# One weight fetch moved to the head of its period, and the GpSimd weight sums begun one period later

## The chip, the cores and the metric

The kernel runs on one core of a Trainium2 chip. The metric is the device time of the whole program in microseconds (us). Before the change it is 1308.43 us, the median of three runs (1307.17 to 1308.57).

## What is computed

The reference has two parts. The first is attention with a threshold over 8 batches of 8 heads, with 576 queries and keys of 64 elements each:

```
scores = q @ k.T / 8
scores = where(scores >= max(scores) - tau, scores, -1e9)
attn   = exp(scores - max) / (sum + 1e-9)
x      = attn @ v            # then (B,H,S,D) -> (4608, 512)
```

The second is a feed-forward layer on the 4608 rows of x: `h = max(x @ w_in, 0)`, then `out = (h * h) @ w_out`, with w_in 512 x 2048 and w_out 2048 x 512. The weights arrive with 64 bits per element, all else with 32.

## The kernel before, in words

**Two stages.** The attention stage runs to about 512 us of the span, and the feed-forward stage fills the rest. The feed-forward stage multiplies with a two-level scheme of seven products in place of eight (49 products of sums of blocks for each layer), so it needs sums of weight blocks and sums of x beside the blocks themselves. The weights must be turned into 32-bit floats first. Both of these are done in the shadow of attention.

**Periods.** Two heads of one batch make a pair (32 pairs). A unit is up to 128 query rows of a pair, and a period `p` of the function `period` handles two units, A and B (the lists stand from L592 on, `period` itself at L619). There are 72 periods with scores, from 0 to 71, and a few before and after that fill and drain the pipeline. A period issues its work in the order of a list of step names, and each engine executes its instructions in exactly that order. `BEGIN_WITH` has lists for periods 0 and 1, `CONVERTING` is the list while weights are converted (periods 2 to 34), and `PLAIN` is the list after that. The steps that matter here are:

- `SA`, `SB`: scores of unit A and B on TensorE (L434). `topA0` to `topB1`: the maximum over keys on VectorE (L452). `powA0` and so on: the exponential on ScalarE (L462). `maskA0` and so on: the threshold, product and row sum on VectorE (L467). `leastA`, `leastB` (L459) and `over` (L474): tiny GpSimd operations that make the threshold and the sum's denominator. `inv`: the reciprocal on VectorE (L477).
- `U`, `V`, `W`: transposes of the weights of attention on TensorE (L380, and L515 for the reciprocal). `eU`, `eV`, `eW`: their copies out of PSUM on ScalarE (L523). `PV`: the product with v on TensorE (L532). `x`: the result out of PSUM, on ScalarE (L657) in converting periods and on VectorE (L659) in plain ones. `xm`: the scaling on GpSimd (L669, converting periods alone).
- `T`, `eT`: the turn (transposes, L398) of a q or a k block of a later pair, and its copies (L403, L411). Behind `eT` the loads of q (L294) or of k and the rests of q (L308, L315, L316) for the pair two ahead are issued. Seven DMAs make one pair's k. The k of pair 2 is turned in period 3, the q of pair 2 in period 2.
- `fetch`: the load of weight chunk `p` in period `p` (L191), 128 x 512 elements of 64 bits, 512 KB. Four places hold raw chunks.
- `c1` to `c6`: the conversion of a chunk. Chunk m has `c1` (ScalarE, L205), `c3` (GpSimd, L219) and `c2` (GpSimd, L212) in period m + 2, and `c4`, `c5` (VectorE, L227 and L235) and `c6` (GpSimd, L245) in period m + 3. The 32 chunks start in periods 2 to 33, so the last one ends in period 34.
- `s1`, `s2`: one sum of weights each on GpSimd (L122 or L125, 128 x 512), in periods for which `sums_due` says yes. From period 60 on only `s1` makes one. The queue of sums holds 44 for w_in and, appended in period 44, 12 for the first block of x.

All loads and stores but the first few are issued by one engine, SyncE (SP), in the order of the text. Each DMA takes one of eight semaphores in turn, so a DMA waits until the one eight places ahead of it has landed.

In the list of period 1 the fetch of chunk 1 stands behind `eT`, and so behind the loads of k for pairs 2 and 3 that `eT` issues. `sums_due` holds from period 35 on, since `max(starts)` is 33 and period 34 still converts.

Of the kernel before, what the change touches and what calls it, by code (L numbers as in the profile page):

```python
# [48 lines left out]
def kernel(  # L49
# [512 lines left out]
    starts = {m + 2: m for m in range(16 + EARLY)}  # L562
# [2 lines left out]

    def sums_due(p):

        return p > max(starts) and not converts(p)

    def sums_step():  # L570
        while summing and next(summing[0], 0) == 0:
# [11 lines left out]
    def converts(p):  # L583
        return is_wide and (has_chunk(p) or has_chunk(p - 1))

    def has_chunk(p):
        return p in starts

    def begun(n):
# [15 lines left out]
            maskA0 maskA1 maskB0 maskB1  # L605
        """.split(),
        1: """
            SA SB T eT fetch over topA0 topA1 leastA inv V topB0 topB1 leastB powA0 powA1 eV W
            powB0 eW maskA0 maskA1 powB1 maskB0 maskB1
        """.split(),  # L610
    }
# [7 lines left out]
    def period(p):  # L619
# [67 lines left out]
        def every(key):  # L687
# [10 lines left out]
            "c3": lambda: convert3(begun(p)), "c4": lambda: convert4(begun(p - 1)),  # L698
            "c5": lambda: convert5(begun(p - 1)), "c6": lambda: convert6(begun(p - 1)),
            "s1": lambda: sums_due(p) and sums_step(), "s2": lambda: sums_due(p) and p < 60 and sums_step(), "fetch": lambda: fetch(begun(p + 2)),  # L700
        }
        steps["over"] = lambda: do(a, "over")
# [536 lines left out]
```

## Time and profile before

| what | us |
|---|---|
| median of three runs | 1308.43 |
| profiled execution, its own time | 1308.95 |
| its span (first to last instruction) | 1307.2 |
| attention stage, up to the first product of the feed-forward stage | 512.5 |
| TensorE busy | 1283.6 (98% of the span) |
| VectorE, ScalarE, GpSimd busy | 1010.1, 846.1, 915.6 |
| granted TensorE clock, mean | 0.995 |

All times of rows are counted from the start of the span. In a timeline a row gives its start, its duration, the engine and line, the operation, out<-in with shapes and a count where several were merged; brackets tell how long the engine was idle before the row and what ended the wait. SPq is SyncE's queue, whose rows are issues of DMAs. A window row gives the busy time of each engine in a stretch (instructions in brackets), then the granted TensorE clock (1.00 is full speed), the share of the DMA engines and their GB/s. A time to landing runs from the start of a DMA's issue to the arrival of its data.

Where the start of a period is spoken of below, it is the start of the first of its four maximum rows (L452) on VectorE. By these rows converting periods last 7.05 to 7.09 us from period 5 to 33 (one of 7.17 apart), and plain ones 6.34 to 7.15 us from period 36 on, in a pattern that returns every nine periods.

### The profile page before, as it was taken

Reading aid. Unit: us, or ns where it says so; the run is one execution under the profiler, and the core shown is the slowest. Engines: PE = TensorE matmul, PEld = TensorE weight load, DVE = VectorE, ACT = ScalarE, POOL = GpSimd, SP = SyncE. Lnnn points to the kernel's source line nnn. Section 1 sums busy time; section 2 is a strip of 40 time slices with the busy share of each in tenths; the row PEclk is TensorE's granted clock in tenths of the full one; section 3 lists DMA queues with packets and bytes.
Section 4 is the critical chain, followed back from the end, with each engine's and each line's share of the span. In section 5 each row is a group of like instructions: output and inputs, shape, how many; then the busy total and the mean of one; then the engine's idle time right before and its main releaser. Section 6 shows DMA issues by size and latency. Waiting matters only on the chain.

```text
span 1307.2 us, 47836 instructions
## 1 busy us (share of the span) xinstructions
PE 1283.6 (98%) x19463; PEld 1158.4 (89%) x19463; DVE 1010.1 (77%) x2431; ACT 846.1 (65%) x1498; POOL 915.6 (70%) x1023
## 2 busy tenths in 40 slices
PE   8899999999999999999999999999999999999998
PEld 5677777777777778999999999999999999999998
DVE  6899999999999996877787778777646654665463
ACT  5999999988999985657665766675523432433240
POOL 2778788765555320978897889768777777777775
PEclk8999999999999999999999999999999999999999
DMA  5665666544433313466656665579645224522511
GB/s 126 165 158 144 169 180 191 147 103 101 94 78 79 81 39 80 140 192 218 195 169 194 215 196 166 176 262 396 226 157 162 72 95 159 161 65 99 161 33 33
DMA packets 247035, 192.12 MB, mean 147 GB/s; under 512 B 97184, under 2 KB 195488, under 8 KB 246816
## 3 DMA queue, kind: packets, MB, share of 16 engines
q1 hardware_dynamic: 245504, 188.66, 48.0%
q8 instruction: 153, 2.51, 0.8%
q14 instruction: 66, 0.54, 0.1%
q10 hardware_dynamic: 1312, 0.41, 0.1%
HBM read 116.65 MB, written 72.35 MB: 145 GB/s over the span
## 4 chain that ended last, share of the span: by engine, by line
PE 88%; ACT 4%; DVE 3%; DMA 2%; issue 1%; SPq 1%; POOL 0%; ACTq 0%; POOLq 0%; DVEq 0%
PE ph L840 29%; PE po L975 29%; PE sc L532 10%; PE sc L434 10%; PE pt L380 5%; DVE arena L452 2%; PE sc L515 2%; PE sc L398 2%; ACT arena L462 2%; ACT arena L523 1%; PE sc L380 1%; DMA wall<-w 1%; DMA arena<-in_q_dram 1%; DMA g<-arena 0%; DMA arena<-in_moe_w_in_dram 0%
## 5 line engine op out<-in xcount | busy, mean ns | idle before, releaser
L125 POOL TENSOR_TENSOR arena<-arena 128x512 f32<-128x512 f32 (+1 forms) x314 | 377.8, 1222 | 134.9 <-DVE arena L125 116.6
L975 PE MATMUL po<-wall,arena 128*128 128x128 f32 x3528 | 395.0, 276 | 1.8 <-ACT arena L752 1.4
L975 PEld LDWEIGHTS po<-wall,arena 128*128 128x128 f32 x3528 | 394.3, 192 | 2.4 <-ACT arena L752 1.8
L840 PE MATMUL ph<-arena,wall 128*128 128x128 f32 x3528 | 394.2, 275 | 0.7 <-DVE arena L659 0.7
L840 PEld LDWEIGHTS ph<-arena,wall 128*128 128x128 f32 x3528 | 394.0, 192 | 0.8 <-issue 0.8
L125 DVE TENSOR_TENSOR arena<-ph,arena 128x512 f32<-128x512 f32 x378 | 256.4, 689 | 86.2 <-PE ph L840 66.3
L122 POOL TENSOR_TENSOR arena<-arena 128x128 f32<-128x128 f32 (+2 forms) x314 | 254.8, 812 | 48.8 <-DMA arena<-w 32.6
L467 DVE SCALAR_TENSOR_TENSOR arena<-arena 128x576 f32<-128x576 f32 x288 | 236.5, 857 | 2.2 <-ACT arena L462 1.3
L125 DVE TENSOR_TENSOR arena<-po,arena 128x128 f32<-128x128 f32 x378 | 108.3, 290 | 167.9 <-PE po L975 163.7
L452 DVE TENSOR_SCALAR_CACHE_REDUCE arena<-sc 128x576 f32<-128x576 f32 x288 | 205.2, 748 | 12.3 <-ACT arena L523 4.1
L462 ACT ACTIVATE arena<-arena 128x576 f32<-128x576 f32 x288 | 208.8, 774 | 8.1 <-DVE arena L452 5.1
L786 ACT COPY c<-arena 128x512 f32<-128x512 f32 (+1 forms) x303 | 173.5, 580 | 50.5 <-DVE arena L122 41.3
L532 PEld LDWEIGHTS sc<-arena 64*64 64x64 f32 x5760 | 159.2, 133 | 36.3 <-DVE arena L452 20.3
L532 PE MATMUL sc<-arena 64*64 64x128 f32 (+1 forms) x5760 | 180.4, 263 | 2.7 <-DVE arena L452 1.1
L434 PE MATMUL sc<-arena 64*64 64x64 f32 (+1 forms) x2304 | 177.5, 417 | 4.8 <-ACT arena L403 2.3
L122 DVE TENSOR_TENSOR arena<-arena,c 128x512 f32<-128x512 f32 (+1 forms) x267 | 174.9, 663 | 6.0 <-ACT c L786 4.0
L523 ACT COPY arena<-pt 128x1024 f32<-128x1024 f32 x144 | 146.2, 1016 | 29.7 <-PE pt L380 28.4
L752 ACT COPY arena<-po 128x128 f32<-128x128 f32 x63 | 16.6, 263 | 186.5 <-PE po L975 183.7
L380 PEld LDWEIGHTS pt<-ident,arena 64*128 64x128 f32 x2304 | 84.0, 140 | 40.9 <-ACT arena L523 28.3
L752 ACT COPY arena<-ph 128x512 f32<-128x512 f32 x63 | 36.6, 581 | 124.2 <-PE ph L840 123.7
L434 PEld LDWEIGHTS sc<-arena 64*64 64x64 f32 x2304 | 74.4, 134 | 42.7 <-issue 15.5
L380 PE MATMUL pt<-ident,arena 64*128 64x64 f32 x2304 | 102.8, 230 | 3.2 <-ACT arena L523 2.2
(51 smaller groups left out, 917.6 us busy)
## 6 DMA issues: line engine op xcount, KB each, us to landing
g<-arena SPq DMA_DIRECT2D x144, 256.0 KB, 2.5
arena<-g SPq DMA_DIRECT2D x144, 256.0 KB, 4.5
w<-arena SPq DMA_DIRECT2D x60, 256.0 KB, 2.4
wall<-w SPq DMA_DIRECT2D x49, 256.0 KB, 5.2
arena<-w SPq DMA_DIRECT2D x44, 256.0 KB, 3.0
arena<-in_v_dram SPq DMA_DIRECT2D x32, 288.0 KB, 3.9
out_dram<-arena SPq DMA_DIRECT2D x70, 128.0 KB, 2.2
arena<-in_q_dram SPq DMA_DIRECT2D x64, 128.0 KB, 3.8
```

Of the source, the lines that this page charges most:

```text
L122: e.tensor_tensor(out=out, in0=x, in1=y, op=ALU.subtract)
L125: e.tensor_tensor(out=out, in0=x, in1=y, op=ALU.add)
L380: made = nc.tensor.transpose(pt[:, r, ts(slot, HALF)], of[rows, :], ident[rows, rows])
L434: made = nc.tensor.matmul(sc[at, ds(to, count)], lhs, kT[rows, ds(at_k, count)], start=True, stop=True)
L452: made = nc.vector.tensor_scalar(out=s[:, j, :], in0=sc[:, ds(at, S)], scalar1=1.0, scalar2=None, op0=ALU.mult, op1=ALU.min, accum_out=nmx ...
L462: nc.scalar.activation(out=w[:, :, j, :], in_=of(j), func=AF.Exp, bias=nmx[:, j : j + 1], scale=-1.0)
L467: nc.vector.scalar_tensor_tensor(out=w[:, :, j, :], in0=of(j), scalar=thr[:, j : j + 1], in1=w[:, :, j, :], op0=ALU.is_le, op1=ALU.mult, a ...
L523: touch("weights", nc.scalar.copy(joined(to), whole(pt, 0, count)), at, 2 * BANK, m)
L532: made = nc.tensor.matmul(sc[ds(u * D, D), ds(5 * j * BANK + row, count)], loaded_v[i][rows, (c - (u != j)) % CH, :], wT[m][rows, ds(weigh ...
L786: nc.scalar.copy(c, y)
L840: nc.tensor.matmul(to[:, j, :], W_IN[m, k][:, ts(j, P)], of[k][:, m - 1, :], start=(not more and j == 0), stop=True, skip_group_check=True,)
L975: nc.tensor.matmul(to, g[:, j, :], w[:, j, :], start=(not more and j == 0), stop=(j == 3), skip_group_check=True)
```

## The change

Two lines change. In the list of period 1, `fetch` moves from the fifth place to the first. In `sums_due`, the bound rises by two, so that the first sums are made in period 36 in place of 35 (period 34 was excluded anyway).

```diff
     def sums_due(p):
-        return p > max(starts) and not converts(p)
+        return p > max(starts) + 2 and not converts(p)
...
         1: """
-            SA SB T eT fetch over topA0 topA1 leastA inv V topB0 topB1 leastB powA0 powA1 eV W
+            fetch SA SB T eT over topA0 topA1 leastA inv V topB0 topB1 leastB powA0 powA1 eV W
             powB0 eW maskA0 maskA1 powB1 maskB0 maskB1
         """.split(),
```

The instructions of TensorE, VectorE and ScalarE keep their order. On SP the issue of chunk 1 moves ahead of fourteen issues, the k loads of pairs 2 and 3, and stands right behind the four q loads of these pairs. On GpSimd the 56 sums stay in their order, and the first of them stands one period later among the tiny operations of attention. The last stands two periods later, since the final sums come one to a period.

## Prediction, made before the changed kernel was run

> **What bounds the kernel now.** First the chain that ended last, by engine:
>
> ```profile
> PE 88%; ACT 4%; DVE 3%; DMA 2%; issue 1%; SPq 1%; POOL 0%; ACTq 0%; POOLq 0%; DVEq 0%
> ```
>
> TensorE carries the end. Work on other engines counts only where TensorE or the chain of attention waits for it, and time saved before 512 us reaches the end, because from there on TensorE is busy throughout (its waits behind 495 us add up to 3.8 us). So I looked for the two places the diff touches in the list of waits. Chunk 1 has one wait to its name, in ScalarE's timeline of period 3:
>
> ```profile
> 30.01 1.01 ACT L523 COPY arena<-pt 128x1024 f32<-128x1024 f32 x1
> 34.35 0.66 ACT L205 ACTIVATE arena<-arena 128x512 f32<-128x512 f32 x1 [3.33 <-DMA arena<-in_moe_w_in_dram]
> 34.91 2.09 ACT L462 ACTIVATE arena<-arena 128x576 f32<-128x576 f32 x3
> ```
>
> ScalarE is free at 31.02 and holds all its later work behind `c1` of chunk 1 (L205) until the chunk lands. TensorE's timeline shows that this is passed on, once through the reciprocal (POOL's `over` stands behind `c3`, which needs `c1`) and once through the copies of `x`:
>
> ```profile
> 33.99 0.34 PE L380 MATMUL sc<-ident,arena 64*128 64x64 f32 x4
> 36.55 0.46 PE L515 MATMUL sc<-ident,arena 64*64 64x64 f32 x16 [2.22 <-DVE arena L477]
> 38.01 1.24 PE L434 MATMUL sc<-arena 64*64 64x512 f32 x12 [1.00 <-ACT arena L657]
> ```
>
> The same hole costs once more. The granted clock (the 1.00 or 0.50 in the windows) falls right after it:
>
> ```profile
> 34.00:38.00 4.00, 0.79 (x24) 0.52 (x20) 1.68 (x6) 3.65 (x10) 2.66 (x5) 1.00 1.05 307
> 39.20:42.60 3.40, 3.40 (x46) 1.90 (x38) 2.75 (x7) 2.81 (x5) 2.66 (x4) 0.50 0.18 39
> 42.60:46.00 3.40, 3.40 (x104) 2.89 (x104) 3.01 (x9) 2.85 (x7) 2.36 (x5) 1.00 0.58 137
> ```
>
> 46 matmuls in 3.4 us at half clock, 104 in the next 3.4. The only other fall inside the kernel (18.7 to 25.5) also follows a stretch with little TensorE work (1.36 us busy of 14 to 18).
>
> The second place is period 35. Its maxima start at 260.50, those of period 36 at 268.51: 8.01 us, where the same place of the nine-period pattern takes 6.52 (period 44) and 6.51 (period 53). GpSimd, VectorE, TensorE there:
>
> ```profile
> 262.24 0.23 POOL L474 TENSOR_SCALAR arena<-arena 128x4 f32<-128x4 f32 x1
> 262.55 1.28 POOL L125 TENSOR_TENSOR wall<-wall 128x512 f32<-128x512 f32 x1
> 263.81 0.29 POOL L459 TENSOR_SCALAR arena<-arena,tau_p 128x2 f32<-128x2 f32 x1
> 264.07 1.29 POOL L122 TENSOR_TENSOR wall<-wall 128x512 f32<-128x512 f32 x1
> ```
>
> ```profile
> 264.14 1.83 DVE L467 SCALAR_TENSOR_TENSOR arena<-arena 128x576 f32<-128x576 f32 x1 [0.78 <-POOL arena L459]
> ```
>
> ```profile
> 266.23 1.51 PE L434 MATMUL sc<-arena 64*64 64x512 f32 x24 [0.90 <-DVE arena L659]
> ```
>
> GpSimd enters the first plain period late, with chunk 31's `c6` and `xm` (260.00 to 262.16). The first sum then stands ahead of `leastA`, the mask waits 0.78 for that, then meets the second sum and takes 1.83 in place of the usual 0.81, and `x` behind it (L659) makes TensorE wait 0.90.
>
> **The fetch, step by step.** SP now:
>
> ```profile
> 16.34 4.42 SPq L308 DMA_DIRECT2D arena<-in_k_dram  x2
> ...
> 24.30 0.60 SPq L316 DMA_DIRECT2D arena<-in_q_dram  x1
> 25.00 1.29 SPq L308 DMA_DIRECT2D arena<-in_k_dram  x2
> ...
> 29.60 1.68 SPq L191 DMA_DIRECT2D arena<-in_moe_w_in_dram  x2
> ```
>
> After the change the chunk takes the place of 16.34. The issue there was held 3.76 (the longest L308); a fetch's own issue takes 0.43 to 1.20, so it ends between 16.8 and 20.1. Fetches land 3.9 to 6.6 after their start (median 4.8), a start at the end of the hold included: 20.2 to 26.7. It is wanted at 31.02, so the wait goes with 4.3 us or more to spare.
>
> What is late next in period 3? ScalarE starts `c1` 3.33 earlier, so `x`'s copies let TensorE begin period 4's scores at 38.01 - 3.33 = 34.68. VectorE's last conversion row ends at 33.45, and its run of rows without idle time, 36.32 to 40.57, then begins at 33.45 and ends at 37.70. TensorE needs 2.36 from the scores through the turn (46.12 to 48.48 in period 5, at full clock): 37.04. So VectorE is later, and period 4's maxima start at 37.70 in place of 41.14: **3.44**. Period 4 lasted 7.56; without half clock I give it the 7.06 of its successors: **0.50**. Together **3.94**. Bounds: at most (10.82 - 7.06) + 0.50 = 4.26, and 3.44 if the clock falls anyway.
>
> What the moved issue pushes back: the seven k DMAs of pair 2, whose last lands at 27.1 now (24.30 + 2.8), wanted by TensorE's turn at 29.80:
>
> ```profile
> 29.80 0.47 PE L398 MATMUL sc<-ident,arena 64*128 64x64 f32 x10
> ```
>
> They slip by one issue (0.43 to 1.20) and by the chunk's 512 KB, an estimated 1.7 us at the 269 to 331 GB/s of 17 to 20 us: 27.5 to 30.0. The slack is 2.7, so I take nothing, and keep 0.2 of loss as the near bound. The q of pair 2 (issued 14.69, lands 6.75 later, TensorE waits 0.44 for it) is ahead of the chunk; shared bandwidth could cost 0 to 1.7, and I take 0, since its row now has a k load in the same place behind it. Pair 3's k (wanted in period 5) and chunk 2 have room: chunk 2 now starts at 30.85, lands 5.0 later and has one fetch less ahead of it, and is wanted at 41.68 - 3.44 = 38.2. The raw chunks have four places, so none is short. SP's eight semaphores come round as before once chunk 1 is passed.
>
> **The sums, step by step.** In period 35 GpSimd goes from `over` (262.47) straight to `leastA` (0.29), done near 262.85. The mask starts when VectorE's fourth maximum ends, 263.36, and takes 0.74, the spacing of masks in an undisturbed run: 264.10. `x` then waits for `PV`, which ends at 264.18, and ends near 264.65, before TensorE comes to need it: the scores follow L515 (264.88) at its spacing of 0.28, at 265.2 in place of 266.23. That is 1.0. Period 36 in turn took 6.94 from scores to scores (266.23 to 273.17) where its successors take 6.58 and 6.51, as it began with VectorE late: 0.4 more, less what the first sums cost there. Taken: **1.3**, between 0.9 (the wait alone) and 1.49 (8.01 - 6.52).
>
> At the other end, 44 + 12 = 56 sums were made as 25 x 2 + 6 and end in period 65; now 24 x 2 + 8, ending in period 67, near 479 us. Their user begins at 512, so 33 us cover them; otherwise the cost would be one sum, 1.3, for each that is left. Periods 66 and 67 gain a sum each: 7.13 and 6.35 without, 7.14 and 6.35 at the same places (57, 58) with three and one. Cost 0, bound 0.2 each (6.50 against 6.68 in periods 69 and 60). GpSimd's tiny operations behind the sums are the same there as in every plain period.
>
> The mask of 1.83 bears on a rule of the Trainium skill (page "SBUF — State Buffer", section "SBUF: two separate sides"): GpSimd and a VectorE operation with two SBUF inputs take a shared port pair as an exclusive lock, and the loser waits for the whole instruction. The trace agrees: 264.14 to 265.36 is the rest of the second sum, and 0.61 is left for the mask. By that rule alone the change only moves collisions.
>
> **Sum.** 3.94 + 1.3 = 5.2 us. The profiled execution: 1308.95 - 5.2 = 1303.7 (span 1302.0, with 1.75 around it). It lies 0.52 above the median of the runs shown, so the predicted median is 1308.43 - 5.2 = **1303.2**.
>
> **Rivals.**
> 1. *The collision moves along* (10%). Period 36 takes over the loss of period 35, as it also holds two sums ahead of its masks. For: a mask beside a sum took 1.83. Against: period 36 with two sums lasted 6.44 and its mask took 1.10, since GpSimd was in time. Gain 3.94 alone: 1304.5.
> 2. *k comes late* (8%). Chunk 1 delays pair 2's k beyond 29.80. For: seven issues behind, one queue of DMAs. If the chunk's issue is held to 20.10 and the first k issue ends only when the chunk has landed, 4.8 to 6.6 later (24.9 to 26.7), k's last lands 7.0 after that, as it does now (20.10 to 27.1): 31.9 to 33.7. TensorE needs it at 30.2 (the last two of the ten transposes): a stall of 1.7 to 3.5, 2.6 in the middle: 1305.8. Against: the first k issue now ends at 20.10, while the first chunk and all four q loads are still under way, so it need not wait for a landing. The Trainium skill ("DMA: Bandwidth & Descriptors", section "Queues, rings and completion order") has descriptors on one engine consumed in ring order, which speaks against this change: by it k comes later by the chunk's transfer, the 1.7 above, and still in time.
> 3. *The wait does not go* (4%), as ScalarE is held by something hidden under it (period 3's maxima, all done at 33.1). Then only the sums count: 1307.1.
> 4. *Slower* (3%). SP is held a second time: the chunk lands at 26.7, the next k issue is held 3.76 more, and k's last lands 7.0 later, at 37.5. TensorE stalls 7.3 from 30.2 on, and the half clock stays (0.50): 7.8 lost in place of 3.94, with 1.3 from the sums: +2.6, 1311.0. It turns slower once k lands behind 34.9 (30.2 + 3.94 + 1.3 - 0.5). Against: of the six k issues behind the first, the longest took 1.49.
>
> **Numbers.** Forecast 75%. This kernel's measurement can tell about 0.2% (2.6 us) from no change. Faster by more than that (below 1305.8): the forecast, rival 1 and over half of rival 2, 0.90. Within: rival 3, the rest of rival 2, 0.07. Slower 0.03. Range: the best case, 4.26 + 1.49, gives 1302.7; the lowest of the runs shown lies 1.26 under their median, so 1301.4. Above, the middle of rival 2, 1305.8.
>
> **What would show it.** Right: no wait at L205 in period 3, maxima of period 4 near 37.7, full clock from 25.5 on, period 35 near 6.6 with a mask of 0.8 and TensorE's 0.90 gone, then the same rows up to 5.2 us earlier. Wrong: a wait of L398 for k near 30, a half-clock window near 39, period 36 near 8.

## The result, and the profile after

The changed kernel takes 1303.86 us (median of five runs, 1302.09 to 1304.45), the kernel before 1308.57 beside it (1307.17 to 1309.65). The ratio is 0.9959, with a 95% interval of 0.9947 to 0.9972: a gain of 4.7 us, between 3.7 and 6.9. The forecast was 1303.2 and a gain of 5.2. The profiled execution took 1302.09 (span 1300.3), the fastest of its five, so it flatters the change, and the account below doesn't rest on it alone. One execution of the kernel before, among the comparisons below, took 2088.8 at a granted clock of 0.556 and is left out of every ratio.

The first product of the feed-forward stage starts at 506.01 in place of 512.47. From there to the first product of the second layer both kernels take 394.03 us. So 6.5 of the 6.9 by which the two profiled spans differ are gained in the attention stage, as the prediction had it.

The chain that ended last, by engine, on the page of the changed kernel:

```profile
PE 91%; ACT 4%; DVE 3%; DMA 2%; issue 1%; POOL 0%; ACTq 0%; POOLq 0%; SPq 0%; DVEq 0%
```

SyncE's queue has gone from 1% to 0%. ScalarE's timeline of period 3 in the changed kernel shows why:

```profile
28.35 1.01 ACT L523 COPY arena<-pt 128x1024 f32<-128x1024 f32 x1
29.26 0.69 ACT L205 ACTIVATE arena<-arena 128x512 f32<-128x512 f32 x1
29.84 2.10 ACT L462 ACTIVATE arena<-arena 128x576 f32<-128x576 f32 x3
```

`c1` (L205) follows the copy at once, with no bracket behind it. TensorE's timeline, same stretch:

```profile
28.14 0.47 PE L398 MATMUL sc<-ident,arena 64*128 64x64 f32 x10
...
32.50 0.34 PE L380 MATMUL sc<-ident,arena 64*128 64x64 f32 x4
32.77 0.46 PE L515 MATMUL sc<-ident,arena 64*64 64x64 f32 x16
33.05 1.36 PE L434 MATMUL sc<-arena 64*64 64x512 f32 x24
```

Both waits that `c1` had caused (2.22 at L515, 1.00 at L434) are gone, and the turn of k (L398) doesn't wait for its data, though the chunk now stands ahead of it on SyncE:

```profile
16.45 1.83 SPq L191 DMA_DIRECT2D arena<-in_moe_w_in_dram  x1
18.32 1.26 SPq L308 DMA_DIRECT2D arena<-in_k_dram  x2
...
22.24 1.44 SPq L316 DMA_DIRECT2D arena<-in_q_dram  x1
...
28.38 0.97 SPq L191 DMA_DIRECT2D arena<-in_moe_w_in_dram  x1
```

The long hold fell on the chunk's issue and was 1.83 in all. The fetches up to 39.2 land 4.6 to 5.9 after their start, where the landing is recorded, and chunk 1 is there at 22.40, 6.9 ahead of `c1`. The windows of the changed kernel (TensorE is the first pair of numbers, the granted clock the third from the end):

```profile
30.00:33.40 3.40, 3.40 (x106) 3.00 (x106) 3.40 (x11) 3.40 (x9) 2.66 (x5) 1.00 1.09 267
36.30:39.70 3.40, 3.28 (x96) 2.80 (x92) 3.40 (x11) 3.31 (x6) 3.16 (x7) 1.00 0.38 82
```

TensorE has no hole, and no half clock follows. Now periods 35 and 36, GpSimd first, then VectorE and TensorE:

```profile
257.19 0.23 POOL L474 TENSOR_SCALAR arena<-arena 128x4 f32<-128x4 f32 x1
257.52 0.29 POOL L459 TENSOR_SCALAR arena<-arena,tau_p 128x2 f32<-128x2 f32 x1
...
261.97 0.23 POOL L474 TENSOR_SCALAR arena<-arena 128x4 f32<-128x4 f32 x1 [2.77 <-DVE arena L467]
262.28 1.28 POOL L125 TENSOR_TENSOR wall<-wall 128x512 f32<-128x512 f32 x1
```

```profile
258.24 0.81 DVE L467 SCALAR_TENSOR_TENSOR arena<-arena 128x576 f32<-128x576 f32 x1
...
264.90 0.81 DVE L467 SCALAR_TENSOR_TENSOR arena<-arena 128x576 f32<-128x576 f32 x1
```

```profile
260.12 1.27 PE L434 MATMUL sc<-arena 64*64 64x512 f32 x24
```

In period 35 `leastA` (257.52) stands right behind `over`; the mask starts at 258.24 without a wait and takes 0.81, and TensorE goes into the scores without its 0.90. The first sum is at 262.28, in period 36, where GpSimd is in time; the mask there (264.90) takes 0.81 as well. Period 35 lasts 6.50 (8.01 before), period 36 lasts 6.44 (6.44 before).

### The profile page after: what moved, and what is told of

It is laid out like the page before. It is cut to its first block, busy times and chain, and to the rows that moved or that the text cites. A ratio compares the mean times of both kernels' runs of the same rounds, so it can differ in the third digit from the quotient of the medians.

```text
span 1300.3 us, 47830 instructions
## 1 busy us (share of the span) xinstructions
PE 1280.6 (98%) x19463; PEld 1157.1 (89%) x19463; DVE 1009.3 (78%) x2431; ACT 846.5 (65%) x1498; POOL 916.7 (71%) x1023
## 4 chain that ended last, share of the span: by engine, by line
PE 91%; ACT 4%; DVE 3%; DMA 2%; issue 1%; POOL 0%; ACTq 0%; POOLq 0%; SPq 0%; DVEq 0%
PE ph L840 30%; PE po L975 29%; PE sc L532 11%; PE sc L434 10%; PE pt L380 6%; DVE arena L452 2%; PE sc L515 2%; PE sc L398 2%; ACT arena L523 1%; ACT arena L462 1%; DMA wall<-w 1%; PE sc L380 1%; DMA g<-arena 0%; ACT arena L403 0%; PE idle L1027 0%
## 5 line engine op out<-in xcount | busy, mean ns | idle before, releaser
L434 PE MATMUL sc<-arena 64*64 64x64 f32 (+1 forms) x2304 | 176.5, 414 | 3.4 <-ACT arena L403 2.3
L434 PEld LDWEIGHTS sc<-arena 64*64 64x64 f32 x2304 | 74.2, 134 | 41.4 <-issue 14.4
```

Of the source, the lines that this page charges most:

```text
L434: made = nc.tensor.matmul(sc[at, ds(to, count)], lhs, kT[rows, ds(at_k, count)], start=True, stop=True)
```

## Experiments

The theory on trial: ScalarE holds all its later work behind `c1` until chunk 1 is there, and that hold, the half clock that follows it and the loss in period 35 are the whole gain. The rivals: it is the order of the DMAs that counts, not the hold; the half clock comes anyway; period 35 loses by the place of the sum in GpSimd's queue alone, or by the ports alone; and k is close to being late. Twelve runs were made, in three groups of four; each is compared with runs of the kernel before on the same chip (medians 1308.19, 1307.51 and 1307.69).

| run | time, median | ratio, 95% interval | `c1` of chunk 1 starts [wait] | from there to period 5 | half clock after 30 us | period 31 | period 35 |
|---|---|---|---|---|---|---|---|
| before (profile) | 1308.57 | 1 | 34.35 [3.33] | 14.35 | yes | 7.09 | 8.01 |
| changed (profile) | 1303.86 | 0.9959 (0.9947–0.9972) | 29.26 | 13.79 | no | 7.36 | 6.50 |
| fetch_alone | 1304.54 | 0.9969 (0.9957–0.9981) | 29.49 | 13.92 | no | 7.39 | 7.99 |
| sums_alone | 1307.58 | 0.9994 (0.9982–1.0005) | 33.87 [4.72] | 14.82 | yes | 7.07 | 6.50 |
| c1_late | 1305.73 | 0.9977 (0.9966–0.9987) | 33.16 | 11.09 | no | 7.34 | 8.00 |
| least_first | 1308.59 | 0.9998 (0.9988–1.0007) | 34.75 [5.61] | 14.67 | yes | 7.05 | 7.63 |
| hot_hole | 1313.75 | 1.0044 (1.0028–1.0059) | 31.86 [0.91] | 16.43 | no | 7.08 | 8.01 |
| three_ahead | 1302.23 | 0.9959 (0.9945–0.9974) | 29.45 | 13.66 | no | 7.08 | 6.50 |
| two_ahead | 1303.12 | 0.9965 (0.9953–0.9978) | 30.15 | 13.99 | no | 7.09 | 6.50 |
| after_again | 1302.77 | 0.9965 (0.9952–0.9978) | 29.14 | 13.98 | no | 8.79 | 6.50 |
| hot_hole2 | 1308.04 | 0.9999 (0.9990–1.0009) | 32.56 [1.80] | 13.93 | no | 7.08 | 8.00 |
| first_only | 1307.32 | 0.9996 (0.9985–1.0007) | 32.56 [3.17] | 14.68 | yes | 7.08 | 7.00 |
| three_again | 1303.24 | 0.9963 (0.9949–0.9976) | 30.17 | 13.94 | no | 7.06 | 6.50 |
| after_third | 1302.59 | 0.9965 (0.9953–0.9978) | 30.28 | 13.88 | no | 7.70 | 6.51 |

All columns from the fourth on are read from one profiled execution each, the lengths from the starts of the maxima as before. Between 10 and 30 us every one of the fourteen profiles has one stretch of half clock, which begins between 16 and 20 us. It lasts 3.4 us in eight of them and 6.8 in six (the profile before, hot_hole, hot_hole2, two_ahead, three_again, after_third). Period 3 starts at 28.46 to 29.27 in the eight and at 29.96 to 30.49 in the six. Both lengths occur with the old and with the new place of the fetch: the three profiles of the changed kernel have 3.4, 3.4 and 6.8. So the shorter periods 1 and 2 of its first profile go with the shorter half clock and not with the change.

**fetch_alone**: the list of period 1 alone.

```diff
-            SA SB T eT fetch over topA0 topA1 leastA inv V topB0 topB1 leastB powA0 powA1 eV W
+            fetch SA SB T eT over topA0 topA1 leastA inv V topB0 topB1 leastB powA0 powA1 eV W
```

> Only the fetch of chunk 1 moves to the head of period 1; the sums begin in period 35 as before. My theory (ScalarE is held by the landing of chunk 1, and a half-clock window follows the hole): no wait at L205 in period 3, periods 3 and 4 last 7.07 each in place of 10.82 and 7.56, so 3.9 to 4.3 us are gained, and period 35 still takes 8.0: about 1304.5 beside 1308.5. Rival (the two parts overlap or one of them brings it all): either the whole 4.7 of both together (1303.9), or next to nothing (1307.5 or more). In the changed kernel periods 1 and 2 were shorter by 1.0 and 0.7 as well: if the moved fetch causes that, it shows here and the gain is up to 5.6; if it is chance from one execution to the next, they may take any value.

**sums_alone**: the bound of the sums alone.

```diff
-        return p > max(starts) and not converts(p)
+        return p > max(starts) + 2 and not converts(p)
```

> Only the sums begin in period 36; the fetch stays behind the k loads. My theory (GpSimd comes late into period 35, and the first sums delay the threshold and the mask): period 35 takes 6.5 in place of 8.0, period 36 stays at 6.4, gain 1.3 to 1.5, about 1307.1 beside 1308.5; the wait at L205 in period 3 stays at 3.3. Rival (the collision moves along to period 36): period 36 takes 7.9, gain 0. Periods 1 and 2 have the order of before: near 7.5 and 8.1 if the order of the DMAs sets them, otherwise any value.

Measured: the fetch alone gains 3.7 us (2.5 to 5.6), and its wait and half clock are gone. The sums alone gain 0.6, with an interval from 2.4 gained to 0.7 lost, so the time doesn't resolve them; the profile does: period 35 is 6.50 long, as in every run that begins the sums later. Why so little of that 1.5 shows in the times of sums_alone isn't settled: its profiled execution has one period of 8.13 (period 28), in which TensorE stands for 0.61 inside `PV` on "issue", that is, on nothing that the profile shows. Period 36 isn't longer for it (6.45), which speaks against the rival that the collision moves along. One thing in fetch_alone was not foreseen. ScalarE's timeline there, `c1` of chunk 2:

```profile
36.95 0.68 ACT L205 ACTIVATE arena<-arena 128x512 f32<-128x512 f32 x1 [0.41 <-DMA arena<-in_moe_w_in_dram]
```

Chunk 2 was late by 0.41, where I had seen room of over 2 us: its fetch waits in SyncE's queue as chunk 1's did, and started at 31.66.

**c1_late**: no DMA is moved. Period 3 gets a list of its own, in which `c1` stands behind `x`, and `c3` behind `leastB`, so neither `x` nor `over` waits for the chunk. The cut shows the new list against `CONVERTING`, which it replaces in period 3.

```diff
-        fetch SA U eU T SB topA0 s1 c1 topA1 topB0 c3 V PV leastA over powA0 topB1
-        powA1 powB0 c4 eT inv x maskA1 maskA0 W leastB maskB0 c5 eV c2 powB1 c6 eW maskB1 xm
+        fetch SA U eU T SB topA0 s1 topA1 topB0 V PV leastA over powA0 topB1
+        powA1 powB0 c4 eT inv x c1 maskA1 maskA0 W leastB c3 maskB0 c5 eV c2 powB1 c6 eW maskB1 xm
```

> No DMA moves and the sums begin in period 35. In period 3 alone, the ScalarE step of chunk 1 (c1) stands behind the copies of x, and its GpSimd successor (c3) behind leastB. The chunk still lands near 34.3. My theory (what counts is that ScalarE's queue is held, not when the chunk lands): the exponentials run from 31.0 on, c1 is reached near 34.4 and waits under 0.5, periods 3 and 4 last 7.1 each, gain 3.4 to 4.3, about 1304.6 beside 1308.5. Rival (the gain of the fetch comes from the order or the load of the DMAs): no gain, 1308.5.

ScalarE's timeline of c1_late:

```profile
32.84 0.43 ACT L657 COPY arena<-sc 128x128 f32<-128x128 f32 x2
33.16 0.70 ACT L205 ACTIVATE arena<-arena 128x512 f32<-128x512 f32 x1
```

The copy of `x` now runs before `c1`, which finds its chunk there. Period 5 starts at 44.25 in place of 48.70, 4.5 earlier, and no half clock follows. So the hold on ScalarE makes the loss, and most of it goes with the fetch left where it was. Not all of it: periods 3 and 4 take 7.47 and 7.66, where 7.1 each was expected. GpSimd reaches `c3` of chunk 1 only at 33.95 (30.04 in the changed kernel), and is late into period 4, where the reciprocal waits 0.48 for `over`. The time gains 2.5 (1.7 to 4.4), where 3.4 to 4.3 was expected, and less than the profile up to period 5 shows. Part of the difference is seen in the profiled execution, in TensorE's timeline inside a run of `PV`:

```profile
133.69 0.32 PE L532 MATMUL sc<-arena 64*64 64x128 f32 x1 [0.92 <-issue]
```

Again "issue", and period 17 lasts 8.12 in place of 7.06. Single long periods like this appear in four of the fourteen profiles (the others are period 28 with 8.13 in sums_alone, hot_hole and first_only), and their cause isn't known. None of the four is the changed kernel, but a lesser one is: in after_third TensorE stands for 0.85 on "issue" in period 7, which lasts 7.49.

**least_first**: the kernel before with a list of its own for period 35, in which the first sum stands behind `leastA`. The second sum stays. The cut shows the start of the list against `PLAIN`, which it replaces there; so does that of first_only.

```diff
-        SA c3 T topA0 over U eU s1 SB topA1 powA1 leastA topB0 powB0 c1 s2 PV c4 V fetch
+        SA c3 T topA0 over U eU SB topA1 powA1 leastA s1 topB0 powB0 c1 s2 PV c4 V fetch
```

> The fetch and the start of the sums are as before. In period 35 alone the first sum stands behind leastA in place of ahead of it. Two causes were named for period 35: the mask waits 0.78 for leastA, queued behind a sum, and then takes 1.83 in place of 0.81 beside the second sum. If the queue is the cause, the mask starts near 263.4 and period 35 loses most of its 1.5: about 1307.2 beside 1308.5. If the sharing of ports between a sum and a mask is the cause, both sums now run back to back over the mask (262.9 to 265.4), the mask ends as late as before, near 266, and nothing is gained: 1308.3 to 1308.6, with period 35 at 7.8 or more.

GpSimd, then VectorE in least_first:

```profile
263.20 0.29 POOL L459 TENSOR_SCALAR arena<-arena,tau_p 128x2 f32<-128x2 f32 x1
263.46 1.28 POOL L125 TENSOR_TENSOR wall<-wall 128x512 f32<-128x512 f32 x1
264.81 1.67 POOL L122 TENSOR_TENSOR wall<-wall 128x512 f32<-128x512 f32 x1
```

```profile
263.92 1.43 DVE L467 SCALAR_TENSOR_TENSOR arena<-arena 128x576 f32<-128x576 f32 x1
...
265.68 1.42 DVE L467 SCALAR_TENSOR_TENSOR arena<-arena 128x576 f32<-128x576 f32 x1
```

`leastA` is in time and the mask no longer waits for it, yet period 35 still takes 7.63: two masks beside sums take 1.43 and 1.42 in place of 0.81, and the second sum 1.67 in place of 1.28. Taking the queue away gives 0.38 of the 1.5.

**first_only**: the other half. In period 35 the first sum stays ahead of `leastA`, and there is no second.

```diff
-        SA c3 T topA0 over U eU s1 SB topA1 powA1 leastA topB0 powB0 c1 s2 PV c4 V fetch
+        SA c3 T topA0 over U eU s1 SB topA1 powA1 leastA topB0 powB0 c1 PV c4 V fetch
```

> As before, but period 35 makes one sum in place of two: the first, which stands ahead of leastA, stays, and the second, which ran beside the mask, is left to period 36 and so on. With the first moved behind leastA period 35 took 7.63. If the two causes add up (8.01 = 6.50 + 0.4 for the queue + 1.1 for the ports), this run has the queue alone: the mask waits about 0.8 for leastA, then takes 0.81 in place of 1.83, and period 35 takes 6.9 to 7.2. If the queue alone were enough, 7.6 or more. Time 0.8 to 1.1 under before by that account.

GpSimd, then VectorE in first_only:

```profile
262.12 1.28 POOL L125 TENSOR_TENSOR wall<-wall 128x512 f32<-128x512 f32 x1
263.37 0.58 POOL L459 TENSOR_SCALAR arena<-arena,tau_p 128x2 f32<-128x2 f32 x2
```

```profile
263.71 0.82 DVE L467 SCALAR_TENSOR_TENSOR arena<-arena 128x576 f32<-128x576 f32 x1 [0.79 <-POOL arena L459]
```

The wait for `leastA` is as it was (0.79), the mask then takes 0.82, and period 35 lasts 7.00. The queue is worth 7.00 - 6.50 = 0.5, the second sum beside the masks 8.01 - 7.00 = 1.0. With least_first's 0.4 and 7.63 - 6.50 = 1.1 the two parts come out the same from both sides, and they add up. Neither moved the time by what the comparison can tell.

**hot_hole**: the kernel before, with 24 transposes that nobody reads, on TensorE, ahead of `W` in period 3. They were to fill the hole, so that only the half clock changes.

```diff
+                keep_busy(24 * (p == 3), sc[:, ds(2 * BANK, P)])
```

> The kernel before, with 24 filler transposes (about 0.136 us each at full clock) put ahead of W in period 3, so that TensorE works through most of the hole while chunk 1 is awaited; what they compute is overwritten. It prices the half clock by itself. In the profiles so far period 5 starts 13.8 to 13.9 us behind c1 of chunk 1 where the clock stays full, and 14.35, 14.66 and 14.82 behind it where a half-clock window follows the hole. If the half clock is a cost of its own, no window near 39, 13.8 to 14.0 here, and 0.5 to 0.9 less than before: about 1307.6. If it costs nothing (hidden under VectorE): 14.4 or more and the time of before, or up to 1 us more for fillers that overrun.

TensorE's timeline of hot_hole (the added lines shift the numbers by one):

```profile
35.71 2.84 PE L1028 MATMUL sc<-ident 128*128 128x128 f32 x24 [1.54 <-ACT arena L658]
```

The fillers write where `x` is copied from, so they waited 1.54 for that copy and then delayed what came after. The half clock is gone, but the run prices the fillers, not the clock, and doesn't answer its question. Why the time is 6.2 us longer is only found in part: the profiled execution, 1310.50 and at the fast end of its runs (1310.26 to 1314.23), reaches the feed-forward stage 1.5 later than the profile before.

**hot_hole2**: the same 24 transposes, now declared as separate from the banks that `x` uses, so that they start as soon as TensorE is free.

```diff
+                for _ in range(24 * (p == 3)):
+                    made = nc.tensor.transpose(sc[:, ds(2 * BANK, P)], ident[:, :], ident[:, :])
+                    touch("turns", made, 2 * BANK, BANK)
```

> The kernel before with 24 filler transposes ahead of W in period 3, as in the run named hot_hole, but the fillers now wait only for the maxima in their own PSUM bank and no longer for the copies of x (there they waited 1.5 for ScalarE and then ran 3.3 us past it, so that the run priced the fillers and not the clock). c1 of chunk 1 still waits 3 to 5.6 for its landing near 34. If the half clock costs by itself: no half-clock window between 30 and 45, period 5 starts 13.7 to 14.1 behind c1 (five profiles without the hole: 13.65 to 14.0) in place of 14.35 to 14.82, and the time is 0.5 to 0.9 under before. If not: 14.3 or more and the time of before.

TensorE's timeline, then windows of hot_hole2:

```profile
33.91 2.84 PE L637 MATMUL sc<-ident 128*128 128x128 f32 x24
```

```profile
32.00:36.00 4.00, 4.00 (x90) 3.83 (x83) 2.87 (x9) 3.44 (x8) 2.42 (x5) 1.00 1.02 290
36.50:39.80 3.30, 3.30 (x75) 2.10 (x77) 2.67 (x6) 2.49 (x4) 2.87 (x3) 1.00 0.26 49
```

The same windows of first_only, whose fetch also stands in the old place and whose `c1` starts at the same 32.56:

```profile
32.00:36.00 4.00, 1.33 (x42) 0.89 (x34) 1.52 (x5) 3.44 (x8) 2.45 (x5) 1.00 0.94 268
36.50:39.80 3.30, 3.30 (x44) 2.53 (x42) 2.23 (x5) 1.90 (x3) 2.85 (x3) 0.50 0.48 104
```

With the hole filled (4.00 busy in place of 1.33) the clock stays at 1.00. From `c1` to period 5 the two take 13.93 and 14.68, so the half clock is worth 0.75 here. In the time that can't be seen: 1308.04, and the interval of a gain is 1.3 to -1.2 us.

**three_ahead** and **two_ahead**: the changed kernel with chunks 1 to 3, or 1 and 2, all loaded at the head of period 1. This presses on the rival that k comes late. The cut is that of three_ahead; two_ahead differs in the chunks named.

```diff
-"fetch": lambda: fetch(begun(p + 2)),
+"fetch": lambda: [fetch(m) for m in ((1, 2, 3) if p == 1 else () if p in (2, 3) else (begun(p + 2),))],
```

> The changed kernel, but chunks 1, 2 and 3 are all fetched at the head of period 1 and none in periods 2 and 3. It prices the rival in which the k of pair 2 comes late. In the two profiles with one chunk ahead, the last k DMA of pair 2 starts at 22.2 and 25.2 and is wanted near 28.2. Two more chunks of 512 KB at 270 to 330 GB/s and two more issues put 4.2 to 5 us on that: landing near 29.5 to 32.5, a wait of TensorE for k in period 3 of 1 to 4 us, periods 3 and 4 at 15 to 18 together in place of 14.2, and 1304.5 to 1307.5 beside 1303.9. If DMAs share the bandwidth so that k does not wait for the chunks ahead of it: no wait, 1303.5 to 1304.

> The changed kernel, but chunks 1 and 2 are fetched at the head of period 1 and none in period 2. With the fetch moved alone, c1 of chunk 2 waited 0.41 in period 4 for its landing at 36.9, so chunk 2 is next in line. One more chunk ahead puts 2.1 to 2.5 us on the k of pair 2, which landed 0.7 to 2 us ahead of its turn: a wait of 0 to 1.5 for k, against up to 0.4 gained at chunk 2. Equal to the changed kernel within 1 us, 1303.5 to 1305, and rather slower than faster.

**after_again**, **three_again**, **after_third**: the changed kernel twice more and three_ahead once more, unedited, to see what comes back.

> The changed kernel once more, for a profile of its own and more runs. Its first profile was the fastest of its runs: periods 1 and 2 were 1 us shorter there than in three other profiles. If that was chance, they take 7.1 to 7.2 each here and the span is near 1302; period 35 takes 6.5 and 36 takes 6.4 again. Time 1303.9, that is 0.6 to 1.5 below the fetch alone (1304.5).

> Three chunks ahead of the k loads once more, beside the changed kernel in the same call. The first run had no wait for k and none for chunks 2 and 3, at 1302.2 against 1302.8 for the changed kernel. In four profiles period 31 was 0.3 to 1.7 longer, where c1 waits for a store of converted weights late in SP's queue; in the two with more chunks ahead it was not. If that is due to the order of the fetches, this run has 7.1 in period 31 and is 0.3 to 1 faster than the changed kernel; if it is chance, the two are equal within 0.5.

> The changed kernel, to stand beside three_again on the same chip. 1302.5 to 1304; period 31 takes 7.3 or more again if its wait belongs to this order of fetches, 7.1 if it is chance.

SyncE's and TensorE's timeline of three_again:

```profile
16.73 2.79 SPq L191 DMA_DIRECT2D arena<-in_moe_w_in_dram  x3
...
23.77 0.60 SPq L316 DMA_DIRECT2D arena<-in_q_dram  x1
```

```profile
29.05 0.47 PE L398 MATMUL sc<-ident,arena 64*128 64x64 f32 x10
```

With 1.5 MB ahead of it, k is still there when TensorE turns it: no bracket. I had expected it to land at 29.5 to 32.5 and to cost 1 to 4 us; the last of its loads landed at 28.34 and cost nothing. In three_ahead there was no room left: 28.31, and the turn starts at 28.33. The order in which the three chunks land (22.2, 23.5 and 25.6 in three_ahead) and k behind them is that of the queue. The Trainium skill ("DMA: Bandwidth & Descriptors", section "Queues, rings and completion order") has descriptors consumed in ring order, and these landings agree; what the order costs is another matter, and here it was nothing. Neither kernel can be told apart from the changed one in time.

After_again showed something else. ScalarE's timeline in period 31, first of the changed kernel's first profile, then of after_again:

```profile
228.23 0.68 ACT L205 ACTIVATE arena<-arena 128x512 f32<-128x512 f32 x1 [0.80 <-DMA w<-arena]
```

```profile
229.51 0.70 ACT L205 ACTIVATE arena<-arena 128x512 f32<-128x512 f32 x1 [2.18 <-DMA w<-arena]
```

`c1` of period 31 waits for the store of the converted chunk 26, whose place it is to overwrite. Period 31 lasts 7.36, 8.79 and 7.70 in the three profiles of the changed kernel, 7.39 in fetch_alone and 7.34 in c1_late, each with such a wait; in all others it lasts 7.05 to 7.09, with no such wait or one of 0.11 (hot_hole). So some of what period 3 gains is given back 190 us later, 0.3 to 1.7, in the mean of the changed kernel's three profiles (7.36 + 8.79 + 7.70) / 3 - 7.07 = 0.9. In the first of them period 32 has a wait of this kind too (0.24) and lasts 7.34, which makes the mean 1.0. What is shown is that the store comes later relative to its period there (it lands 1.1 to 2.6 us after the period's start, 0.3 after to 1.9 before in the others). That the order of the fetches causes it isn't shown: c1_late moves no DMA and has the wait, two_ahead and three_ahead gain as much in period 3 and haven't, and hot_hole2, with the old order, has one of 1.09 in period 22. Nor does the time show it: three_again, without the wait, was expected to be 0.3 to 1 faster than after_third, and took 1303.24 against 1302.59.

## Why the prediction held, step by step

- **The wait at `c1`: right.** It goes, by the mechanism given: c1_late removes it without touching a DMA. Rival 3, that it stays, is refuted.
- **Its size: 4.3 in place of 3.44.** In the four profiles with the fetch and `c1` in their old places and nothing added to TensorE (before, sums_alone, least_first, first_only), `c1` starts at 33.88 in the mean; in the four with the changed order and no further fetch (the changed kernel three times, fetch_alone), at 29.54. The step that fell short is "ScalarE starts `c1` 3.33 earlier": the bracket was read as the size of the loss. But a bracket runs from the moment ScalarE is ready to the landing, and the two vary apart from each other. ScalarE was ready at 31.02 in the profile before and at 29.14 to 29.39 in the other three. The fetch was issued at 29.60, 29.45, 30.36 and 27.75, after a k load ahead of it had held SyncE for 3.76, 3.04, 3.65 and 1.96, and the chunk was there 4.4 to 4.8 later. So the four brackets are 3.33, 4.72, 5.61 and 3.17. In the profile before ScalarE came late and hid part of the wait: the early half clock lasted 6.8 there and 3.4 in the other three, and periods 1 and 2 took 15.62 together, against 13.81 to 14.40. For the one profile that the forecast used, its 3.94 for wait and half clock was nearly right: periods 3 and 4 lose 10.82 + 7.56 - 7.07 - 7.09 = 4.2 (period 3 takes 7.07, where 37.70 - 30.32 = 7.38 was forecast). The other three put that at 4.2 to 6.3.
- **The half clock: right that it costs by itself, 0.75 in place of 0.50.** From `c1` to period 5 the four profiles with it take 14.63 in the mean, the four of the changed order 13.89, a difference of 0.74, and the pair above gives 0.75. The forecast compared period 4 alone. That fits the profile before, where period 4 takes 7.56 and the whole comes to 14.35 - 13.89 = 0.46. In the other three the clock falls earlier: period 4 takes 7.07 or 7.08, and the loss lies between `c1` and period 4 (7.59 to 7.74, against 6.70 in the changed kernel).
- **k of pair 2 and q of pair 2 at 0: right.** From 14 to 46 us no turn (L398) waits for a DMA in the three profiles of the changed kernel, so rivals 2 and 4 did not come about. The room is not large, though: where its landing is recorded, the last of pair 2's seven loads is there 1.0 (fetch_alone) to 5.5 (after_third) before the turn with one chunk ahead of it, and 0.02 (three_ahead) to 0.7 (three_again) with three.
- **Chunk 2's slack: too large.** It was worked out as 2.3 (38.2 less 35.9); in fetch_alone it was -0.41. This cost less than the comparison can tell.
- **The sums: right, 1.5 in place of 1.3.** Of the bounds 0.9 to 1.49 the upper one is met (8.01 - 6.50). The wait in the queue (0.4 to 0.5) and the masks beside the second sum (1.0 to 1.1) make it up. The sums' later end cost nothing: the first product of the feed-forward stage waits 0.7, for L659, as it did.
- **Rival 1, that the collision moves on: refuted.** Period 36 lasts 6.44 to 6.45 with the sums begun in it, and 6.43 to 6.44 with them begun in period 35. By the rule of the Trainium skill on the shared ports ("SBUF — State Buffer", section "SBUF: two separate sides"), a mask beside a sum waits for it; least_first agrees, where its two masks take 1.43 and 1.42, the 0.82 and 0.81 that the sums still run and 0.61 after that. The collision doesn't move along because GpSimd is in time in period 36: the first mask starts at 264.90, when the last sum (263.79, 1.28 long) has only 0.17 left, and takes its usual 0.81; the later masks meet none.
- **Missing: periods 31 and 32.** The 1.0 that comes back was nowhere in the sum.

The account by the profiles is 4.34 + 0.74 + 1.5 - 1.0 = 5.6, the three comparisons give 4.7, 4.7 and 5.1, the forecast was 5.2. The mechanisms were right, but the term sizes were off by up to 1.0 and nearly cancelled, so that the sum came so near is in part luck. The remaining 0.5 to 0.9 lies within the interval of 3.7 to 6.9 and isn't explained.

## What to carry to other kernels

A bracket in one profile tells how early the waiting engine was as much as how late the data were: where a transfer's landing is set by a queue, price its removal from the landing and the next dependency, and look at how far the periods ahead vary, in more than one profile. On an in-order engine an early load and a later place for the instruction that needs it remove the same wait; the second moves no traffic, but delays what hangs on that instruction (here 1.0 of the loss stayed). After a gain, follow every ring of buffers to its end: the changed kernel waits for a store 190 us later in all three of its profiles.

## What the runs showed of the hardware

- The half clock follows stretches that are partly busy. In each profile the changes of the granted clock lie multiples of 3.41 us apart (before: 18.71, 25.54, 39.19, 42.60). Cut the time at these points into stretches of 3.41 us. Before 50 us, those at full clock that a fall followed had TensorE busy for 0.17 to 0.61 of their length (before: 1.70 us from 15.30 on, 1.63 from 35.77). Two with 0.58 were followed by none (before from 32.36, hot_hole from 34.28), so the runs give no sharp bound. A stretch at half clock was the last where TensorE was busy for 0.97 of it or more (fetch_alone: 3.32 us from 19.01). Another followed at 0.87 or less (before: 2.97 from 18.71; sums_alone: 1.86 from 35.28; least_first: 0.89 from 35.18). So the half clock lasted 3.4 or 6.8 us. Where the 3.41 us begin differs between executions: the clock first becomes full at 4.1 to 7.0 us.
- A VectorE mask that starts while a GpSimd sum runs ends 0.61 us after that sum: 1.22 (before), 0.82 and 0.81 (least_first) and 0.48 (before, period 36) of the sum were left, and the masks took 1.83, 1.43, 1.42 and 1.10. With 0.17 left (changed kernel, period 36) it took its usual 0.81. The sum can lose too: in least_first the second one started at 264.81, during a mask that ended at 265.35, and took 1.67 in place of 1.28.
- One issue of a DMA can hold SyncE for several times the usual 0.4 to 0.6 us. In thirteen of the fourteen profiles the issue that stands at 15.8 to 16.8 us is held for 1.45 to 3.76, whether it is a load of k (3.76 in the profile before) or the chunk (1.83 in the changed kernel, 3.60 in fetch_alone).
- TensorE can stand for 0.9 us inside a run of like matmuls with no wait shown, and a period is then 1.06 longer (c1_late, period 17). The runs of one kernel differ by up to 7.7 us (1304.9 to 1312.6 for the kernel before in the first group).
